# Attention and a maxout FFN on one core: groups of four heads in four 32-column TensorE tiles, 128-token output tiles, 1 KB loads, casts on GpSimd and in the weight DMA

## The chip, the cores and the metric

The kernel runs on one NeuronCore of one Trainium2 chip. The metric is the device time in microseconds (us) of one execution; medians of several executions are given. In one core's profile, PE is TensorE's matmul stream, PEld its weight loads, DVE is VectorE, ACT is ScalarE, POOL is GpSimd, SP is SyncE, which only issues DMAs here. "FFN" is the part with the weights: three up-projections, their maximum, and the output projection. "AV" is the product of the exponentials with v. A "visit" to the scores is a run of score matmuls between two runs of other matmuls: they use half of the array's 128 rows each, two at a time (row tiling), while the others use all rows, so the array changes its tiling mode on the way in and out. A column tile is a strip of 32 of the array's 128 columns. PSUM is the memory that the matmuls write (the tiles stp, av, p_i, op_ps and trT). "Streamed" means matmuls that follow one another without a wait; with 448 columns their starts are then 0.19 us apart.

## The reference

```python
# q, k, v: (8, 12, 448, 64) float32; w1, w2, w3, w_out: (768, 768) float32
scores = (1 / sqrt(64)) * q @ k.transpose(0, 1, 3, 2)
m = max(scores, axis=-1, keepdims=True)
e = exp(scores - m)
attn = e / (sum(e, axis=-1, keepdims=True) + exp(-m) + 1e-09)
x = (attn @ v).transpose(0, 2, 1, 3).reshape(8 * 448, 768)
h = maximum(maximum(x @ w1, x @ w2), x @ w3)
out = h @ w_out                       # (3584, 768) float32
```

The extra `exp(-m)` is a "1" in the denominator once the maximum is left out, as both kernels do.

## The kernel before

It takes two heads (a pair) at a time. The 448 tokens are four chunks of 112 partitions. Loads of q, k and v bring blocks of six heads in rows of 256 bytes (one head's 64 floats). All weights go through one float32 staging tile and are cast by ScalarE:

```python
wstage = ctx.enter_context(tc.tile_pool(name="wstage", bufs=1))
for i, w in enumerate((moe_w1, moe_w2, moe_w3, moe_w_out)):
    wst = wstage.tile([128, NDC, DFF], FP32, tag="wst")
    nc.sync.dma_start(out=wst, in_=w.rearrange("(dc p) f -> p dc f", p=128))
    wt = cpool.tile([128, NDC, DFF], MMDT, name=f"w{i}")
    nc.scalar.copy(out=wt, in_=wst)
```

For each pair, VectorE casts q and k, TensorE transposes them, the *previous* pair's AV product is computed (the weights are `[v | ones]`, 128 columns, so that the denominator comes out in the upper 64 rows), and then come four score visits, each of two 64-row matmuls (one head in each row half of the array). One FFN piece of the batch before is put after the first head's AV, and one after the scores:

```python
for hh in range(2):                                  # previous pair
    av = ps1.tile([128, 512], FP32, tag="bank1")
    for c in range(NCH):
        nc.tensor.matmul(out=av[:, 0:S], lhsT=v_sb[0:kk, vslot, c, :],
                         rhs=eT_all[0:kk, parq, hh, c, :], ...)
    nc.scalar.activation(out=lnd_sb, in_=av[D : 2 * D, 0:S], func=AF.Ln)
    nc.scalar.activation(out=rb_sb, in_=lnd_sb, func=AF.Exp, scale=-1.0)
    nc.vector.tensor_tensor(out=xTp_[...], in0=av[0:D, 0:S], in1=rb_sb, op=ALU.mult)
    if hh == 0:
        moe_next()
# ... cut ...
for c in range(NCH):                                 # this pair
    stp = ps2.tile([SC, 2, 512], FP32, tag="bank2")  # two buffers
    for hh in range(2):
        nc.tensor.matmul(out=stp[:, hh, 0:S], lhsT=kT2[hh*D : hh*D+D, ts(c, SC)],
                         rhs=qT2[hh*D : hh*D+D, :], start=True, stop=True)
    nc.scalar.activation(out=eT_all[0:SC, parp, :, c, :], in_=stp[:, :, 0:S],
                         func=AF.Exp, scale=scale)
moe_next()
```

## Time and profile before

| | before |
|---|---|
| time, median of 3 (range) | 471.24 us (471.17 to 475.31) |
| TensorE busy, share of the span | 419.1 us, 89% |
| one batch in the steady state | 51.76 us, of which TensorE is busy 49.97 |
| first up-projection with the third weight | 77.40 us |
| tail: from the eighth batch's first up-projection to the end | 35.7 us |

The page of the kernel before: busy time, then the span in 40 slices of 11.8 us (busy tenths, granted TensorE clock in tenths, busy tenths of the DMA engines, GB/s), then the DMA packets.

```profile
span 471.8 us, 6238 instructions
...
PE 419.1 (89%) x2400; PEld 212.3 (45%) x2400; DVE 269.6 (57%) x594; ACT 279.8 (59%) x392; POOL 0.7 (0%) x6
...
PE   2788724999999999999999999999999999998996
...
PEclk9965665999999999999999999999999999999999
...
GB/s 185 221 262 1 266 197 287 254 124 100 193 91 87 8 218 73 172 1 144 150 135 42 57 225 70 118 1 204 89 177 0 75 101 1 1 27 92 1 0 117
DMA packets 137053, 53.87 MB, mean 114 GB/s; under 512 B 130368, under 2 KB 130368, under 8 KB 137024
```

TensorE is nearly full from the eighth slice on. Before, it is busy for 42.9 of 77.4 us, much of it at half clock. Nearly all packets are under 512 bytes. The fourth slice moves 1 GB/s: the loads stand still although the weights are not yet there.

Two stretches of the kernel before, the start and one batch of the steady state (length; then busy us and instructions of PE, PEld, DVE, ACT, POOL; granted clock; DMA share; GB/s):

```profile
0.00:77.40 77.40, 42.90 (x173) 15.43 (x173) 28.58 (x68) 51.70 (x59) 0.70 (x6) 0.70 0.90 195
...
287.29:339.05 51.76, 49.97 (x302) 25.88 (x302) 33.05 (x74) 32.52 (x49) 0.00 (x0) 1.00 0.54 107
```

In the steady state no engine but TensorE is near its limit. To shorten a batch one has to take matmul time away, or the 1.8 us of idle time.

The timeline of TensorE in the kernel before, part of one pair (start, length to the modelled end of the last matmul, line, what, count, and in brackets the idle time before and what ended it):

```profile
293.60 0.59 PE L303 MATMUL stp<-qT_2789,kT_2791 64*112 64x448 f16 x4
294.12 0.93 PE L151 MATMUL p_i<-xT_b,w_112 128*128 128x448 f16 x4
295.24 0.40 PE L303 MATMUL stp<-qT_2789,kT_2791 64*112 64x448 f16 x2 [0.19 <-ACT eT_all L310]
295.56 0.55 PE L151 MATMUL p_i<-xT_b,w_112 128*128 128x448 f16 x2
295.95 0.54 PE L151 MATMUL p_i<-xT_b,w_116 128*128 128x448 f16 x2
296.50 0.40 PE L303 MATMUL stp<-qT_2789,kT_2791 64*112 64x448 f16 x2
296.82 0.93 PE L151 MATMUL p_i<-xT_b,w_116 128*128 128x448 f16 x4
```

The starts are what to read, since ends are modelled. A visit of four score matmuls takes from 293.60 to 294.12, 0.52 us, and one of two takes 0.32; streamed, a pair of them is worth 0.19. Eight matmuls need three visits here, because there are two score buffers and each must wait for its exponential (the wait in brackets). Over a batch this makes 18 or 19 visits.

The chain of waits of the kernel before, in order of time, up to the first matmul with the third weight (start, length, what):

```profile
1.17 8.13 DMA k__97<-in_k_dram
...
43.65 3.92 ACT w_112 L115
47.57 1.62 ACT eT_all L310 x2
...
60.74 3.93 ACT w_116 L115
64.69 8.60 DMA wst<-in_moe_w_dram
73.31 4.04 ACT w_120 L115
77.40 2.42 PE p_i L151 x6
```

The second weight's load is issued at 47.59 us, after the first weight's cast, which starts at 43.65, and the third's at 64.69 after the second's cast. The casts stand in ScalarE's queue behind exponentials.

### The profile page before, as it was taken

How to read it: one execution, taken by the hardware profiler on the slowest of the kernel's cores; microseconds unless marked ns; L12 is line 12 of the kernel's file. 1: busy time of each engine (PE TensorE's matmuls, PEld its weight loads, DVE VectorE, ACT ScalarE, POOL GpSimd, SP SyncE). 2: the span in 40 equal slices, each digit the busy share in tenths (PEclk: the TensorE clock that was granted, in tenths of full speed). 3: DMA queues.
4: the chain of work that ended last, by engine and by line, in shares of the span. 5: the costliest groups of instructions: out<-in, count | busy, mean ns of one | idle time of the engine just before them, and what ended most of it. 6: DMA issues, size and time to landing. Idle time of an engine off the chain costs nothing.

```text
span 471.8 us, 6238 instructions
## 1 busy us (share of the span) xinstructions
PE 419.1 (89%) x2400; PEld 212.3 (45%) x2400; DVE 269.6 (57%) x594; ACT 279.8 (59%) x392; POOL 0.7 (0%) x6
## 2 busy tenths in 40 slices
PE   2788724999999999999999999999999999998996
PEld 1222202445444554445454554456444544455454
DVE  5434322575666666656566666667566556555453
ACT  3778843766765567457855576556844776556300
POOL 0000000000000000000000000000000000000000
PEclk9965665999999999999999999999999999999999
DMA  9990979974945093906672293708490340002003
GB/s 185 221 262 1 266 197 287 254 124 100 193 91 87 8 218 73 172 1 144 150 135 42 57 225 70 118 1 204 89 177 0 75 101 1 1 27 92 1 0 117
DMA packets 137053, 53.87 MB, mean 114 GB/s; under 512 B 130368, under 2 KB 130368, under 8 KB 137024
## 3 DMA queue, kind: packets, MB, share of 16 engines
q1 hardware_dynamic: 137024, 53.48, 53.1%
q8 instruction: 18, 0.29, 0.3%
q14 instruction: 11, 0.09, 0.1%
HBM read 42.47 MB, written 11.01 MB: 113 GB/s over the span
## 4 chain that ended last, share of the span: by engine, by line
PE 74%; ACT 17%; DMA 4%; issue 3%; DVE 2%; SPq 0%; ACTq 0%
PE p_i L151 31%; PE av L272 15%; PE op_ps L172 12%; PE stp L303 12%; ACT eT_all L310 10%; ACT rb_sb L282 2%; DVE xT_b L283 2%; PE trT L242 2%; DMA wst<-in_moe_w_dram 2%; PE trT L237 2%; DMA k__97<-in_k_dram 2%; ACT lnd_sb L280 2%; ACT w_120 L115 1%; ACT w_116 L115 1%; ACT w_112 L115 1%
## 5 line engine op out<-in xcount | busy, mean ns | idle before, releaser
L310 ACT ACTIVATE eT_all<-stp 112x896 f16<-112x896 f32 x192 | 164.3, 908 | 11.1 <-PE stp L303 9.9
L280 ACT ACTIVATE lnd_sb<-av 64x448 f32<-64x448 f32 x96 | 50.5, 539 | 135.9 <-PE av L272 135.6
L283 DVE TENSOR_TENSOR xT_b<-av,rb_sb 64x448 f16<-64x448 f32 x96 | 59.0, 615 | 81.1 <-ACT rb_sb L282 80.7
L272 PE MATMUL av<-eT_all,v_sb 112*128 112x448 f16 (+1 forms) x384 | 100.6, 379 | 5.3 <-ACT eT_all L310 2.3
L161 DVE TENSOR_TENSOR hT_b<-hT_b,p_i 128x448 f16<-128x448 f16 x96 | 59.6, 620 | 40.8 <-PE p_i L151 38.0
L151 PE MATMUL p_i<-xT_b,w_120 128*128 128x448 f16 x288 | 64.6, 357 | 11.7 <-ACT w_120 L115 10.3
L172 PE MATMUL op_ps<-w_124,hT_b 128*112 128x384 f16 x384 | 73.7, 331 | 0.0
L151 PE MATMUL p_i<-xT_b,w_116 128*128 128x448 f16 x288 | 67.0, 358 | 5.1 <-ACT w_116 L115 5.1
L151 PE MATMUL p_i<-xT_b,w_112 128*128 128x448 f16 x288 | 69.5, 357 | 1.4 <-DVE xT_b L283 1.4
L172 PEld LDWEIGHTS <-hT_b 128*112 128x112 f16 x384 | 46.3, 129 | 21.7 <-issue 10.3
L282 ACT ACTIVATE rb_sb<-lnd_sb 64x448 f32<-64x448 f32 x96 | 53.3, 569 | 1.1
L272 PEld LDWEIGHTS <-v_sb 112*128 112x128 f16 (+1 forms) x384 | 34.3, 101 | 35.6 <-issue 13.9
L151 PEld LDWEIGHTS <-w_120 128*128 128x128 f16 x288 | 28.3, 99 | 40.3 <-ACT w_120 L115 11.1
L179 DVE TENSOR_SCALAR o_sb<-op_ps 112x384 f32<-112x384 f32 x64 | 35.4, 554 | 16.4 <-PE op_ps L172 14.7
L151 PEld LDWEIGHTS <-w_116 128*128 128x128 f16 x288 | 27.2, 99 | 31.9 <-ACT w_116 L115 5.4
L151 PEld LDWEIGHTS <-w_112 128*128 128x128 f16 x288 | 25.0, 98 | 30.8 <-issue 13.0
L159 DVE CAST hT_b<-p_i 128x448 f16<-128x448 f32 x48 | 29.6, 617 | 10.0 <-PE p_i L151 9.6
L115 ACT CAST w_120<-wst 128x4608 f16<-128x4608 f32 x1 | 4.0, 4032 | 8.6 <-DMA wst<-in_moe_w_dram 8.6
L237 PE MATMUL trT<-ident_86,q_133 112*128 112x112 f16 x4 | 0.9, 294 | 6.6 <-DVE q_133 L223 6.6
L229 DVE CAST k_749<-k__453 112x512 f16<-112x512 f32 x1 | 0.4, 426 | 8.3 <-DMA k__453<-in_k_dram 8.3
L75 DVE MEMSET ones_f_91<- 128x4096 f32 x1 | 3.5, 3472 | 1.7 <-PEq L336 1.7
L254 DVE TENSOR_SCALAR v_sb<-v__99 112x256 f16<-112x256 f32 x6 | 1.5, 290 | 5.0 <-PE av L272 3.9
(507 smaller groups left out, 313.6 us busy)
## 6 DMA issues: line engine op xcount, KB each, us to landing
out_dram<-o_sb SPq DMA_DIRECT2D x32, 336.0 KB, 3.1
wst<-in_moe_w_dram SPq DMA_DIRECT2D x3, 2304.0 KB, 9.7
wst<-in_moe_w_out_dram SPq DMA_DIRECT2D x1, 2304.0 KB, 8.6
q__95<-in_q_dram SPq DMA_DIRECT2D x1, 672.0 KB, 5.4
k__97<-in_k_dram SPq DMA_DIRECT2D x1, 672.0 KB, 8.1
v__99<-in_v_dram SPq DMA_DIRECT2D x1, 672.0 KB, 9.7
q__101<-in_q_dram SPq DMA_DIRECT2D x1, 672.0 KB, 9.8
k__103<-in_k_dram SPq DMA_DIRECT2D x1, 672.0 KB, 10.6
```

The source lines that it names most:

```text
L115: nc.scalar.copy(out=wt, in_=wst)
L151: nc.tensor.matmul(out=p_i[:, 0:S], lhsT=w_sb[i][:, dc, ts(fc, 128)], rhs=xTp[:, dc, :], start=(dc == 0), stop=(dc == NDC - 1),)
L159: nc.vector.tensor_copy(out=hTp[:, fc, :], in_=p_i[:, 0:S])
L161: nc.vector.tensor_tensor(out=hTp[:, fc, :], in0=hTp[:, fc, :], in1=p_i[:, 0:S], op=ALU.max)
L172: nc.tensor.matmul(out=op_ps[0:SC, 0:NW], lhsT=hTp[:, fc, ts(t, SC)], rhs=wout_sb[:, fc, ts(nh, NW)], start=(fc == 0), stop=(fc == NFC - 1),)
L179: nc.vector.tensor_scalar(out=o_sb[:, ts(nh, NW)], in0=op_ps[0:SC, 0:NW], scalar1=1.0 / LAMBDA, scalar2=None, op0=ALU.mult,)
L272: nc.tensor.matmul(out=av[:, 0:S], lhsT=v_sb[0:kk, vslot, c, :], rhs=eT_all[0:kk, parq, hh, c, :], start=(c == 0), stop=(c == NCH - 1),)
L280: nc.scalar.activation(out=lnd_sb, in_=av[D : 2 * D, 0:S], func=AF.Ln)
L282: nc.scalar.activation(out=rb_sb, in_=lnd_sb, func=AF.Exp, scale=-1.0)
L283: nc.vector.tensor_tensor(out=xTp_[(h % HD2) * D : (h % HD2) * D + D, h // HD2, :], in0=av[0:D, 0:S], in1=rb_sb, op=ALU.mult,)
L303: nc.tensor.matmul(out=stp[:, hh, 0:S], lhsT=kT2[hh * D : hh * D + D, ts(c, SC)], rhs=qT2[hh * D : hh * D + D, :], start=True, stop=True,)
L310: nc.scalar.activation(out=eT_all[0:SC, parp, :, c, :], in_=stp[:, :, 0:S], func=AF.Exp, scale=scale,)
```

## The change

The intent: use four heads together so that the AV product fits four 32-column tiles of the array, with one Ln and one Exp for four heads; load more bytes per packet; take the casts from VectorE and ScalarE.

```diff
-            out=q12_, in_=q[bb, hb*HB : (hb+1)*HB].rearrange("h (c p) d -> p (h c) d", p=SC)
+            # token p*4 + c: the four chunks of one partition are 1 KB in a row
+            out=t.rearrange("p h c d -> p h (c d)"),
+            in_=src[b].rearrange("(h g) (p c) d -> g p h (c d)", g=NG, c=NCH)[g],
 ...
-        nc.sync.dma_start(out=wst, in_=w.rearrange("(dc p) f -> p dc f", p=128))
-        nc.scalar.copy(out=wt, in_=wst)
+                nc.gpsimd.dma_start(out=w_sb[i][hh * 32 : hh * 32 + 32], in_=src[hh])  # casts
 ...
-            nc.vector.tensor_copy(out=q16, ...)          # k16 and v alike
+            nc.gpsimd.tensor_copy(out=q16, ...)
 ...
+        def col_tiled(weights):
+            bank = ps1.tile([128, 512], FP32, tag="bank1", name="av")
+            for c in range(NCH):
+                for hh in range(GH):                      # GH = 4
+                    nc.tensor.matmul(
+                        out=bank[32 * hh : 32 * hh + 32, 0:S],
+                        lhsT=weights(hh, c), rhs=eT[:, hh, c, :],
+                        start=(c == 0), stop=(c == NCH - 1))
+            return bank
+        den = col_tiled(lambda hh, c: ones16[:, :])
+        nc.scalar.activation(out=lnd, in_=den[:, 0:S], func=AF.Ln, bias=one_b)
+        nc.scalar.activation(out=rb, in_=lnd, func=AF.Exp, scale=-1.0)
+        for hf in range(2):
+            num = col_tiled(lambda hh, c: v16[:, hh, c, hf * 32 : hf * 32 + 32])
+            nc.vector.tensor_tensor(out=xT[b][:, 2*g + hf, :], in0=num[:, 0:S], in1=rb, op=ALU.mult)
 ...
+    cast_group(0)
+    for i in range(4): load_weight(i)                    # 13 DMAs issued by GpSimd
+    transpose_group(0); cast_group(1)
+    visits = [(pr, cs) for pr in range(2) for cs in ((0, 1), (2, 3))]
+        for vi, (pr, cs) in enumerate(visits):           # per group of 4 heads
+            scores_visit(i, pr, cs)                      # 4 matmuls, then 2 Exp
+            moe(per_visit)                               # an even share of FFN pieces
+            if vi == 0 and i > 0: av_group(i - 1)
+            if vi == 2 and i + 1 < NI: transpose_group(i + 1)
```

The output projection takes 128 tokens at a time over two batches (7 tiles instead of 8 of 112). Not shown in the cut: q and k of a pair leave PSUM in one VectorE copy instead of two, and casts and transposes run one group ahead.

## The prediction

> **What bounds it now.** From about 80 to 440 us the kernel repeats every 51.76 us, once per batch (chain of waits: the same up-projection at 235.54, 287.29 and 339.05 us). In one period (busy time by stretch) PE is busy 49.97 us, DVE 33.05, ACT 32.52, at full granted clock: TensorE bounds it. Streaming per batch, from that period's timeline: up-projection 108 matmuls x 0.19 us = 20.4; output 48 x 0.1625 = 7.8; AV 48 x 0.19 = 9.1; scores 24 row-tiled pairs x 0.19 = 4.6; transposes 48 x 0.05 = 2.4; sum 44.3. The other 7.4 us are short waits for exponentials (0.2 to 0.5 us) and 0.25 to 0.3 us around each of some 18 visits to the row-tiled scores. The Trainium skill (TensorEngine Tiling, Key Properties) says changing tiling mode drains TensorE; the trace agrees: a lone pair takes 0.32 us instead of 0.19.
> The start is slow: the first up-projection with the third weight begins at 77.40 us (timeline). One staging tile makes each weight wait for the ACT cast of the one before (issues at 16.5, 47.6, 64.7 us); 130368 packets are under 512 B. After the last period comes a tail of 31 us.
>
> **What changes, per batch.**
> - AV: 144 matmuls of 32 columns, in fours. If four run together: 36 x 0.2 us (the transposes already issue a load and a matmul every 0.05 us) = 7.2 instead of 9.1.
> - Output on 128 tokens: 42 matmuls, 6.8 instead of 7.8.
> - 12 score visits instead of 18, plus 3 AV visits: 15 x 0.27 = 4.1, plus 1 us of waits, instead of 7.4.
> - Period: 20.4 + 6.8 + 7.2 + 4.6 + 2.4 + 5.1 = 46.5 us. Seven periods save 37 us.
> - ACT falls to about 24.5 us per batch (6 Ln and Exp instructions, not 24), DVE to 25. Neither was critical. GpSimd: 15 casts per batch, an estimate of 10 to 20 us from DVE's 0.42 us at half to quarter speed; hidden.
>
> **Start.** Weights no longer wait for ACT or staging. About 14 MB (three weights, five groups) at 250 to 300 GB/s (peak now 287) puts the third weight at about 50 us instead of 77.
>
> **Time.** 50 + 7 x 46.5 + 34 (end of attention, tail) = 410; with stalls 412 us. Range 394 to 440. Faster by over 2%: 0.93; within 2%: 0.03; slower: 0.04.
>
> **What would show it.** The chain repeats every 46 to 47 us; 16-matmul AV blocks last 0.8 us, four starting within each 0.2 us; ACT and DVE near 200 us busy each; packets under 512 B nearly gone; first up-projection with the third weight at 45 to 60 us; no long wait on GpSimd after the start.
>
> **What would make it wrong.** Column tiles that serialise: the skill (same page, Restrictions) says column tiling disables Fast Weight Load. If one column tile's weight load waits for another tile's matmul, AV costs 27 us per batch and the kernel is slower. The skill (TensorE: Matmul & The Clock Gate, Part 3) gives 2.38x for three column tiles, so partial overlap is possible: each 0.05 us per round costs 13 us in all. Casting DMAs below 200 GB/s, or GpSimd held by issuing thirteen of them before it casts group 1, would push the start to 60 to 75 us.

## The result, and the profile after

The changed kernel takes 392.77 us (392.72 to 393.51, 3 runs) against 471.24. The ratio is 0.8314, 95% interval 0.8261 to 0.8368. Ratios in this document are the mean time of one kernel's runs over that of the other's runs of the same rounds, so not quite the ratio of the medians quoted. Executions over 1.5% slower than the fastest of the same kernel are left out of the means. Below, "before" in each set of runs was between 471.17 and 473.59 us (medians of 7 runs on the same chip).

The same parts of the page, after (slices of 9.8 us):

```profile
span 390.9 us, 7477 instructions
...
PE 363.1 (93%) x3120; PEld 180.1 (46%) x3120; DVE 174.8 (45%) x298; ACT 194.5 (50%) x241; POOL 129.7 (33%) x139
...
PE   2409999999999999999999999999999999999995
...
PEclk9999999999999999999999999999999999999998
...
GB/s 196 272 240 236 239 285 268 250 85 187 143 47 96 198 152 96 134 71 201 143 47 96 162 189 96 117 74 216 49 3 0 82 82 0 2 0 123 2 0 162
DMA packets 41202, 49.24 MB, mean 126 GB/s; under 512 B 2256, under 2 KB 37584, under 8 KB 41168
```

TensorE is full from the fourth slice on, and lost 56 us of busy time. ScalarE and VectorE lost 85 and 95 us, and GpSimd took up 129. Small packets are nearly gone.

The stretches after: the start, and two batches (the output tiles make batches alternate, so two are one period):

```profile
0.00:53.85 53.85, 30.78 (x280) 13.68 (x281) 9.24 (x18) 27.64 (x36) 33.08 (x44) 1.00 1.09 242
...
139.44:227.92 88.48, 88.48 (x783) 44.10 (x780) 43.53 (x74) 48.68 (x61) 30.36 (x31) 1.00 0.46 124
```

A batch now takes 88.48 / 2 = 44.24 us instead of 51.76, and TensorE is busy in all of it. Before, 49.97 of 51.76 were busy, so 5.7 us of the saving are matmul time (with the cost of visits in it) and 1.8 us idle time.

TensorE's timeline after, around one AV block:

```profile
236.85 0.59 PE L166 MATMUL stp<-qkT 64*112 64x448 f16 x4
237.37 1.31 PE L225 MATMUL p_i<-xT,w_113 128*128 128x448 f16 x6
238.52 1.30 PE L225 MATMUL p_i<-xT,w_114 128*128 128x448 f16 x6
239.75 0.94 PE L195 MATMUL av<-eT,ones_109 112*32 112x448 f16 x16
240.51 1.69 PE L195 MATMUL av<-eT,v_2646 112*32 112x448 f16 x32
242.13 0.59 PE L166 MATMUL stp<-qkT 64*112 64x448 f16 x4
242.65 1.31 PE L225 MATMUL p_i<-xT,w_115 128*128 128x448 f16 x6
```

The 48 AV matmuls take from 239.75 to 242.13, 2.38 us. One after another at 0.19 us they would take 9.1. In the trace four start within 10 ns (239.747, .750, .753 and .757), and the next four at 239.946: four column tiles run together. There are no brackets: nothing waits. Each score visit has four matmuls and takes 0.52 us, and there are 12 per batch.

The chain of waits after, over the start:

```profile
29.09 0.57 POOL k_0_163 L127
...
32.80 2.73 PE av L195 x43
...
35.90 6.57 ACT eT L175 x8
...
50.51 0.52 PE stp L166 x4
51.03 2.38 PE p_i L225 x12
53.40 0.52 PE stp L166 x4
53.92 2.19 PE p_i L225 x11
```

The first up-projection starts at 50.96 us, and that with the third weight at 53.85 instead of 77.40. The weights no longer stand in the chain; GpSimd's cast of the second group does, at 29.09 us. TensorE waits 13.3 us for that group's casts, because GpSimd first issues its weight DMAs (one at 1.3 us, the other twelve from 12.8 to 28.5; from the tenth of the thirteen on it waits for earlier ones to land). The granted clock of 1.00 in the line of the start above is no measurement up to 33.48 us, where the trace's first clock record stands.

**Where the 81 us of the two spans (471.8 and 390.9) went.** Reading the start of each batch's first up-projection in both traces: up to the second batch's start 125.89 against 94.22, 31.7 us (one period of 7.5 and 24 of start); six further batches 310.1 against 263.5, 46.6 us; the tail 35.7 against 33.2, 2.5 us.

### The profile page after: what moved, and what is told of

Its sections match the earlier page's. It is cut to its first block, busy times and chain, and to the rows that moved or that the text cites. A ratio compares the mean times of both kernels' runs of the same rounds, so it can differ in the third digit from the quotient of the medians.

```text
span 390.9 us, 7477 instructions
## 1 busy us (share of the span) xinstructions
PE 363.1 (93%) x3120; PEld 180.1 (46%) x3120; DVE 174.8 (45%) x298; ACT 194.5 (50%) x241; POOL 129.7 (33%) x139
## 4 chain that ended last, share of the span: by engine, by line
PE 89%; ACT 2%; POOL 0%; DVE 0%; issue 0%
PE p_i L225 43%; PE op_ps L246 15%; PE av L195 15%; PE stp L166 12%; PE trT L148 2%; PE trT L144 2%; ACT eT L175 2%; ACT rb L208 0%; POOL k_0_163 L127 0%; DVE o_sb L253 0%; ACT lnd L206 0%
## 5 line engine op out<-in xcount | busy, mean ns | idle before, releaser
L175 ACT ACTIVATE eT<-stp 112x896 f16<-112x896 f32 x192 | 164.6, 916 | 126.7 <-PE stp L166 126.7
L235 DVE TENSOR_TENSOR hT<-hT,p_i 128x448 f16<-128x448 f16 x96 | 59.7, 621 | 68.4 <-PE p_i L225 68.3
L225 PE MATMUL p_i<-xT,w_114 128*128 128x448 f16 x288 | 62.9, 353 | 0.0
L225 PE MATMUL p_i<-xT,w_113 128*128 128x448 f16 x288 | 62.8, 353 | 0.0
L225 PE MATMUL p_i<-xT,w_115 128*128 128x448 f16 x288 | 62.5, 353 | 0.0
L166 PE MATMUL stp<-qkT 64*112 64x448 f16 x384 | 60.2, 383 | 1.9 <-ACT eT L175 1.9
L246 PE MATMUL op_ps<-w_116,hT 128*128 128x384 f16 x336 | 59.0, 327 | 0.0
L211 DVE TENSOR_TENSOR xT<-av,rb 128x448 f16<-128x448 f32 x48 | 27.7, 620 | 46.3 <-ACT rb L208 46.3
L253 DVE TENSOR_SCALAR o_sb<-op_ps 128x384 f32<-128x384 f32 x56 | 31.3, 558 | 34.2 <-PE op_ps L246 34.0
L233 DVE CAST hT<-p_i 128x448 f16<-128x448 f32 x48 | 30.0, 625 | 32.6 <-PE p_i L225 32.6
L246 PEld LDWEIGHTS <-hT 128*128 128x128 f16 x336 | 30.8, 98 | 27.0 <-issue 8.1
L153 DVE COPY qkT<-trT 128x896 f16<-128x896 f16 x48 | 27.8, 617 | 29.6 <-PE trT L148 29.6
L144 PE MATMUL trT<-ident_104,q_0_162 112*128 112x112 f16 x4 | 0.9, 294 | 13.3 <-POOL q_0_162 L124 13.3
```

The source lines that it names most:

```text
L153: nc.vector.tensor_copy(out=qkT, in_=trT)
L166: nc.tensor.matmul(out=stp[:, hh, 0:S], lhsT=qkT[hh * D : hh * D + D, 1, ts(c, SC)], rhs=qkT[hh * D : hh * D + D, 0, :], start=True, stop= ...
L175: nc.scalar.activation(out=st["eT"][:, 2 * pr : 2 * pr + 2, c, :], in_=stp[:, :, 0:S], func=AF.Exp, scale=scale,)
L211: nc.vector.tensor_tensor(out=xT[b][:, 2 * g + hf, :], in0=num[:, 0:S], in1=rb, op=ALU.mult)
L225: nc.tensor.matmul(out=p_i[:, 0:S], lhsT=w_sb[i][:, dc, ts(fc, 128)], rhs=xT[b][:, dc, :], start=(dc == 0), stop=(dc == NDC - 1),)
L233: nc.vector.tensor_copy(out=dst, in_=p_i[:, 0:S])
```

## The experiments

Fifteen kernels were run. All gave correct results. The names beginning with a_ are edits of the kernel after, those with b_ of the kernel before. "Period" is the mean time per batch from the third to the seventh batch's first up-projection.

### Do four column tiles need the order of the program?

a_serial issues all four chunks of one head before the next head:

```diff
-            for c in range(NCH):
-                for hh in range(GH):
+            for hh in range(GH):
+                for c in range(NCH):
```

> The changed kernel, with the AV matmuls of one head issued in a row (head outside, chunk inside), so that neighbours use the same 32-column tile. Theory (tiles overlap because neighbours in the queue use different column tiles): an AV block of 48 grows from 2.38 us to about 48 x 0.19 = 9.1 us, and the time by 24 x 6.7 = 161 us, to about 550 us. Rival (a 32-column matmul is simply short, the order does not matter): about 393 us.

Measured: 397.94 us (one look, state unknown), period 44.35. Nothing was serialised; the 5 us more are nearly all in the start (first up-projection at 55.46 us instead of 50.96). The AV block of a_serial in TensorE's timeline:

```profile
244.68 0.97 PE L195 MATMUL av<-eT,ones 112*32 112x448 f16 x16
245.45 1.72 PE L195 MATMUL av<-eT,v 112*32 112x448 f16 x32
247.10 0.40 PE L166 MATMUL stp<-qkT 64*112 64x448 f16 x2
```

The block takes from 244.68 to 247.10, 2.42 us. The built program has the heads one after another, yet in the trace four matmuls start 13 ns apart (244.681, .695, .708 and .721), and the next at 244.881, .895, .908 and .921. Since a single column tile takes a new matmul only every 0.19 us, those four must be of different heads: a matmul that waits for its own column tile does not hold those behind it that go to other tiles. (The trace does not name the tile, so this is read from the times.) In the kernel after the four are 3 ns apart, here 13, four times as far, as four issues lie between. So the overlap does not rest on the loop order. The theory that it does fell. The rival had the time nearly right (about 393 us), but not the reason: if 32-column matmuls were simply short, they would start evenly and not in fours.

### What is the AV shape worth, and what else did it carry?

a_fullav puts back `[v | ones]` of 128 columns with Ln and Exp for each head. a_avspread does the same, but puts two heads' AV after each of two score visits instead of four heads' after one.

```diff
+        for hh in range(GH):                       # a_avspread: for hh in heads
+            av = ps1.tile([128, 512], FP32, tag="bank1", name="av")
+            for c in range(NCH):
+                nc.tensor.matmul(out=av[:, 0:S], lhsT=v16[:, hh, c, :], rhs=eT[:, hh, c, :], ...)
+            nc.scalar.activation(out=lnd, in_=av[D : 2 * D, 0:S], func=AF.Ln, bias=one_b[0:D])
+            nc.scalar.activation(out=rb, in_=lnd, func=AF.Exp, scale=-1.0)
-            if vi == 0 and i > 0: av_group(i - 1)
+            if vi < 2 and i > 0: av_group(i - 1, (2 * vi, 2 * vi + 1))      # a_avspread
```

> The changed kernel with AV as before: one 128-column matmul per head and chunk, values and ones side by side, and Ln and Exp per head on 64 partitions (8 instructions a group instead of 2). Theory (TensorE streaming bounds the period, ScalarE has room): a block is 16 x 0.19 = 3.03 us instead of 2.38, so 24 x 0.65 = 16 us more, 405 to 412 us, and no long waits for exponentials. Rival (the relief of ScalarE removed the waits of before): waits return, 3 us or more per batch on top, 430 us or more.

> a_fullav (full-width AV, Ln and Exp per head) with the four heads of a group dealt out over two score visits, two each, instead of all four in one place. ScalarE's work is the same as in a_fullav. In a_fullav the chain of waits ran through four Ln, four Exp and the exponentials queued between them once per group, and the period was about 48.4 us. Theory (not ScalarE's load but four accumulators released one after the other by its queue): period near 44.24 + 1.95 = 46.2 us, time 405 to 418 us. Rival (ScalarE's load): period stays at 48 us or more, 425 us or more.

Measured: a_fullav 434.08 us (ratio 0.9181, interval 0.9124 to 0.9237), period 48.45. a_avspread 422.26 us (0.8954, 0.8923 to 0.8986), period 46.67. The full width costs 46.67 - 44.24 = 2.43 us per batch if it is spread, and 1.78 more if eight Ln and Exp instructions stand together in ScalarE's queue: over the run TensorE waits 10.0 us for exponentials before score matmuls in a_fullav and 3.2 in a_avspread. Both times were longer than expected because the start grew too (57.8 and 59.3 us to the first up-projection). So the rival's 430 us for a_fullav came about, though with 1.78 us per batch from the queue and not 3; a_avspread came out between its theory (405 to 418) and its rival (425 or more), with a period near the theory's 46.2. The four runs of a_fullav range from 428.93 (the profiled one) to 435.84 us (the one counted as slow), so its time is less certain than its period. That the 2.43 is the width itself, the distances of starts show: AV takes 9.65 us per batch in a_avspread against 7.15 in the kernel after.

### What is a score visit worth?

a_visit1 sends one chunk per visit, 24 visits per batch instead of 12, with as many matmuls.

```diff
-    visits = [(pr, cs) for pr in range(2) for cs in ((0, 1), (2, 3))]
+    visits = [(pr, cs) for pr in range(2) for cs in ((0,), (1,), (2,), (3,))]
```

> The changed kernel with one chunk per score visit: 24 visits per batch instead of 12, one feed-forward piece after each. Theory (a visit to the row-tiled scores costs TensorE about 0.25 us beyond its streaming, whatever its length): 12 x 0.25 = 3 us per batch, period 47.2 us, time 413 to 419 us. Rival (the cost lies in waits for exponentials, which one-chunk visits do not add): below 400 us.

Measured: 414.43 us (0.8789, 0.8760 to 0.8818), period 47.17. A stretch of it, columns as before:

```profile
139.40:186.00 46.60, 46.60 (x389) 21.65 (x387) 21.52 (x37) 25.11 (x30) 14.93 (x15) 1.00 0.43 122
```

Twelve more visits cost 2.93 us, 0.244 us each, with no wait in it: TensorE is busy throughout. The Trainium skill (TensorEngine Tiling, Key Properties) says that changing the tiling mode drains TensorE; this run gives the price of one more visit, that is of a change into the mode and one out of it. By that price, six or seven fewer visits than before are worth an estimated 1.5 to 1.7 us per batch.

### Can the kernel before have the same by order alone?

b_visits puts the old score matmuls in two visits of four, with FFN pieces between. b_even also deals the FFN in 26 even pieces. b_look also casts and transposes one pair ahead.

```diff
+            scores((0, 1))          # four matmuls, then two Exp
+            moe_next()              # b_even, b_look: moe(per_visit), an even share
+            prepare(it + 1)         # b_look only: casts and transposes of the next pair
             # ... AV of the previous pair ...
-            for c in range(NCH): ...
+            scores((2, 3))
             moe_next()
```

> The kernel before, with only the order changed: scores of chunks 0 and 1, a piece of the feed-forward part, AV, then scores of chunks 2 and 3, another piece. Instructions and their sizes are unchanged, so ScalarE has the same load. Theory (visits to the scores and waits for the exponentials cost 7.4 us per batch because of the order): 12 visits instead of some 18 and nearly no waits give a period near 47.5 us instead of 51.76 and a time near 440 us (range 435 to 450). Rival (ScalarE's load makes the waits): at most 2% faster, 462 us or more.

> b_visits with the feed-forward part cut into 26 pieces (18 up-projections, 8 half output tiles) and dealt out evenly by columns over the 12 visits, as the changed kernel does; all instructions otherwise unchanged. Theory (in b_visits 5 us per batch are the last pair, which has no feed-forward left to fill the waits): the period falls from 49.4 to about 47.5 us, waits for exponentials nearly vanish, 435 to 442 us. Rival (ScalarE's load per batch, unchanged at 32 us, makes the waits): 450 us or more.

> b_even with casts and transposes done one pair ahead of their scores (six value slots instead of four), as the changed kernel does by group. Instructions and sizes per engine as in the kernel before. Theory (order alone makes the waits): period 44.3 + 12 x 0.25 = 47.3, up to 47.8 us, time 434 to 443 us. Rival (the load of ScalarE and VectorE, 32 and 33 us per batch, makes them): period 49 us or more, 450 us or more.

Measured: b_visits 452.95 us (0.9573, 0.9523 to 0.9623), period 49.44. b_even 458.22 (0.9684, 0.9626 to 0.9742), period 50.22. b_look 452.75 (0.9569, 0.9530 to 0.9608), period 49.63. Order alone is worth 2.3, 1.5 and 2.1 us per batch, and none of the three reached the 47.3 to 48 us hoped for; the times of b_even and b_look are those of their rivals (450 us or more), that of b_visits lies between its theory (435 to 450) and its rival (462 or more). In b_visits FFN work has run out by the last pair of a batch. Here is its timeline there:

```profile
315.72 0.54 PE L297 MATMUL av<-eT_all,v_sb 112*128 112x448 f16 x2
316.72 0.92 PE L297 MATMUL av<-eT_all,v_sb 112*128 112x448 f16 x4 [0.45 <-ACT eT_all L275]
```

b_even cured that and met another wait instead, 9.1 us in all before score matmuls for VectorE's copies of kT. b_look cured that too; what is left in a batch of it is 1.0 us of idle time (TensorE is busy 48.63 of 49.63) and waits shorter than 150 ns, which come up again under b_pool below.

### Where did the start come from?

b_wdma replaces staging and ScalarE's cast in the kernel before by casting DMAs; b_wdma2 holds these by a tiny copy until block 0 has landed.

```diff
-        nc.sync.dma_start(out=wst, in_=w.rearrange("(dc p) f -> p dc f", p=128))
-        nc.scalar.copy(out=wt, in_=wst)
+        nc.gpsimd.tensor_copy(out=wt[0:SC, 0, 0:8], in_=blocks[(0, 0)][2][:, 0, 0:8])  # b_wdma2 only
+        nc.gpsimd.dma_start(out=wt, in_=w.rearrange("(dc p) f -> p dc f", p=128))
```

> The kernel before, with only the weights loaded by casting DMAs from the GpSimd queue, without staging and ScalarE casts. Theory (the start of before is the chain of one staging tile): the first up-projection with the third weight moves from 77 to about 50 us, the period stays 51.76 us, the time is about 445 us (440 to 455). Rival (the start is bound by 256-byte loads): the third weight is not usable before 65 us and the time is 460 us or more.

> The kernel before with casting weight DMAs, as in b_wdma, but held back until the first block of q, k and v has landed (a tiny GpSimd copy from it into each weight tile goes ahead; its bytes are then overwritten). In b_wdma the weights, issued at 1 to 5 us, pushed the first k from 8 to 32 us. Theory (staging chain): with the first block landed first, batch 0 starts near 12 us as before, the third weight is there by about 55 us, 440 to 455 us. Rival (the start of before is bound by something else, so that the weights do not matter): 465 us or more.

Measured: b_wdma 472.66 us (0.998, 0.9933 to 1.0028): nothing gained. GpSimd issues the weights at once, and they share the DMA engines with the first loads: the first k landed after 31.9 us instead of 8.1, and VectorE stood 25.9 us for it. Both theory and rival of b_wdma had left this out, though the time is the rival's. The skill (DMA: Bandwidth & Descriptors, Issuing engines are not separate DMA queues) says just this, that DMAs of all issuers run on the same 16 engines and interleave. b_wdma2 took 460.04 us (0.972, 0.9653 to 0.9787): the same period (51.76), and a second batch that starts at 112.72 instead of 125.89, so 13.2 us of the start. That is between its theory (440 to 455 us) and its rival (465 or more). A wait of 11.0 us for v is still in it, since blocks 1 and 2 now land late.

a_load256 puts 256-byte rows back in the kernel after (in four DMAs per tensor, one per head, which is a second difference; the rows of the output go back to the order of before with it, a third).

```diff
-                in_=src[b].rearrange("(h g) (p c) d -> g p h (c d)", g=NG, c=NCH)[g],
+            rows_in = src[b].rearrange("(h g) (c p) d -> g h p c d", g=NG, c=NCH)[g]
+            for h_ in range(GH):
+                nc.sync.dma_start(out=t[:, h_], in_=rows_in[h_])
```

> The changed kernel with q, k and v loaded in 256-byte pieces as before (token order by chunk, one DMA per head); nothing else changed. Theory (in the steady part transfers are hidden, at the start they are not): period 44.2 us as before, the start later by 5 to 15 us, 398 to 408 us. Rival (load size does not matter): within 3 us of 393.

Measured: 407.61 us (0.8643, 0.8617 to 0.8669). The period is 44.24, unchanged; the first up-projection starts at 65.93 us instead of 50.96. The page of a_load256:

```profile
GB/s 156 199 199 202 206 212 194 203 203 115 185 192 93 93 176 163 92 127 105 190 107 90 93 191 146 94 93 155 146 1 2 39 117 2 2 0 109 11 0 156
DMA packets 141428, 49.27 MB, mean 121 GB/s; under 512 B 134736, under 2 KB 137808, under 8 KB 141392
```

While the start is bound by loads the DMA engines move 194 to 212 GB/s, against 236 to 285 in the kernel after. The skill (DMA: Bandwidth & Descriptors, Why small descriptors are slow) puts the fixed cost of a 256-byte packet at 3 cycles of 11, 27%; the rates here, about a fifth lower (on average 202 against 256 GB/s), agree with that order of size, though the two other differences are in them too. The steady state needs 86 to 124 GB/s and does not notice.

a_dvestart moves the casts of groups 1 to 3 and the scaling of group 0's v to VectorE, to get GpSimd out of the chain that the start shows.

```diff
-    cast_group(1)
+    cast_group(1, nc.vector, nc.vector)        # groups 2 and 3 alike; v of group 0 too
```

> The changed kernel, with the casts of groups 1 to 3 (and the values of group 0) on VectorE, so that GpSimd issues the weight DMAs without holding group 1 back (13.3 us wait of TensorE now). Theory (start bound by that wait, then by the landing of the weights at about 45 us): the first up-projection moves from 51 to about 43 to 46 us and the time to 384 to 388 us. Rival (the start is bound by the weights' landing alone): 391 to 393 us.

Measured: 407.09 us (0.8607, 0.8557 to 0.8657), worse: the first up-projection starts at 64.21 us. GpSimd, freed of casts, issued the weights from 8.6 us on instead of 12.8, so q, k and v landed later (v of the third group at 29.8 us instead of 21.9), and VectorE, whose instructions ran in the order of the program, stood before casts whose data were missing while the copies and products that TensorE needed were behind them (TensorE's longest waits for VectorE: 5.7, 4.0 and 3.8 us). Both theory and rival were wrong. The wait for GpSimd had held the weights back and kept VectorE's queue free; the run changed both at once, so it does not say which of the two mattered more.

### All of it but the matmul shapes

b_all is b_look with 1 KB loads and the held casting DMAs. b_pool is b_all with the casts of q and k and the scaling of v on GpSimd. It has what the kernel after has, except the AV and output shapes, one Ln and Exp for four heads, the joint copy of q and k, and groups of four.

```diff
-            nc.vector.tensor_copy(out=q16, ...)        # b_pool: k16 and v_sb alike
+            nc.gpsimd.tensor_copy(out=q16, ...)
```

> b_look with 1 KB loads and with casting weight DMAs held back until the first block has landed; casts stay on VectorE, AV and output tiles stay as before. Theory: period as in b_look, first up-projection of batch 0 at 50 to 58 us and of batch 1 one undisturbed period later, 415 to 425 us; what then remains to the changed kernel, 7 to 8 times about 3 us, is the matmul shapes. Rival (the casts on GpSimd or ScalarE's relief are needed too): 430 us or more.

> The kernel before with everything of the changed kernel except its matmul shapes and its joint Ln and Exp: order, pieces and look-ahead of b_look, 1 KB loads and gated casting weight DMAs of b_all, and now the casts of q and k and the scaling of v on GpSimd. Theory: the 1.8 us per batch that b_look keeps above its matmuls (49.63 against some 47.8) and b_all's late start come from VectorE's in-order queue, which holds casts that wait for loads in front of copies that TensorE needs. Then the period falls to 47.6 to 48.4 us, the first up-projection with the third weight starts below 56 us, and the time is 418 to 430 us. Rival: VectorE's load is not the reason, and what is left comes from Ln and Exp for each head in ScalarE's queue and from the batch boundary. Then the period stays 49.2 to 49.9 us and only the start moves: 430 us or more.

Measured: b_all 442.54 us (0.9354, 0.9301 to 0.9406), period 49.62; b_pool 433.30 us (0.9164, 0.9132 to 0.9196), period 49.62. One batch of the steady state of b_all, columns as before:

```profile
211.27:260.89 49.62, 48.62 (x303) 25.59 (x301) 33.12 (x74) 32.61 (x49) 0.00 (x0) 1.00 0.47 112
```

And one of b_pool:

```profile
259.60:309.20 49.60, 48.60 (x302) 25.59 (x300) 26.57 (x50) 32.62 (x48) 16.80 (x24) 1.00 0.49 117
```

And its TensorE over one pair:

```profile
260.22 1.68 PE L321 MATMUL av<-eT_all,v_sb 112*128 112x448 f16 x8
261.83 0.59 PE L288 MATMUL stp<-qT,kT 64*112 64x448 f16 x4
262.35 2.44 PE L144 MATMUL p_i<-xT_b,w 128*128 128x448 f16 x12
264.72 0.69 PE L288 MATMUL stp<-qT,kT 64*112 64x448 f16 x4
265.34 2.44 PE L144 MATMUL p_i<-xT_b,w 128*128 128x448 f16 x12
```

b_all kept its theory's period, but not its start (50 to 58 us) and time (415 to 425), which is its rival's. From b_all to b_pool VectorE lost 6.5 us of work per batch, and the period did not move. VectorE's casts are therefore not what keeps the steady state of the old shapes above its matmuls: that theory fell, and the rival's numbers fit. The casts matter at the start: the first up-projection starts at 51.19 us instead of 59.54, and TensorE's waits before transposes fall from 24.0 us, all for VectorE (15.8 for products and 8.2 for casts in its queue), to 16.1 us, 15.9 of them for GpSimd's casts.

### A kernel that beats both

a_densum sums the four chunks of exponentials on VectorE, so that the denominators need 4 matmuls instead of 16 per group. a_best does this from the fourth group on, and puts casts between the weight DMAs in GpSimd's queue.

```diff
+            add_chunks(i, pr, cs[0] // 2)          # a_best: if i >= 3
-        den = col_tiled(lambda hh, c: ones16[:, :])
+        for hh in range(GH):
+            nc.tensor.matmul(out=den[32 * hh : 32 * hh + 32, 0:S], lhsT=ones16[:, :],
+                             rhs=st["sums"][hh // 2][:, hh % 2, :], start=True, stop=True)
-    for i in range(4): load_weight(i)
-    transpose_group(0); cast_group(1)
+    load_weight(0); load_weight(1)                 # a_best only
+    transpose_group(0); cast_group(1); load_weight(2)    # w_out after group 2's casts
```

> The changed kernel, with the four chunks of exponentials added on VectorE, so that the denominators need 4 matmuls a group instead of 16. Theory (TensorE streaming bounds the period; VectorE is busy 43.5 of 88.5 us): 24 x 3 rounds x 0.19 = 13.7 us less, 377 to 383 us. Rival (VectorE's six additions a group, 0.5 to 0.9 us each, delay the copies out of PSUM): 390 us or more.

> a_densum with two mends of the start: the first three groups take denominators from all chunks (in a_densum TensorE waited 4.4 us for the sums there), and GpSimd casts group 1 after the first two weights' DMAs instead of after all four. Theory: steady saving of 1.7 us per batch kept (12 us), the first up-projection at 44 to 48 us instead of 51: 374 to 381 us. Rival (the start is bound by the bytes to be landed, in whatever order): first up-projection at 50 us or later, 380 us or more.

Measured: a_densum 388.44 us (0.8213, 0.8166 to 0.8260): the period falls to 42.53, 1.71 less, as three times 0.19 for three groups; but the first up-projection starts at 57.48 us, as TensorE waits 4.4 us at once for VectorE's sums and the start is stretched, so the time fell between theory and rival. a_best 372.95 us (0.7922, 0.7887 to 0.7957): period 42.53, first up-projection at 45.28, TensorE busy in 95% of the span. That is 20 us less than the kernel after.

## Why the prediction was right or wrong

The kernel is faster by far, as predicted, and by the predicted mechanisms. The number was too high: 412 us predicted, 392.77 measured, just below the range's lower end of 394.

**The step that failed** is the term "12 score visits instead of 18, plus 3 AV visits: 15 x 0.27 = 4.1, plus 1 us of waits", 5.1 us in the sum of 46.5. Measured in the kernel after:

| per batch, us | predicted | measured: rate from the trace times count |
|---|---|---|
| up-projection | 20.4 | 20.43 |
| output | 6.8 | 6.83 |
| AV (3 blocks of 2.38) | 7.2 | 7.14 |
| scores, streaming (24 x 0.19) | 4.6 | 4.6 |
| transposes | 2.4 | 2.4 |
| visits and waits | 5.1 | 3.0 |
| sum | 46.5 | 44.4 |

The rows add up to 0.2 us more than the 44.24 of the trace. The 3.0 is 12 x 0.52 for the visits, plus 12 x 0.11 for the slower up-projection group after each (2.38 us for twelve matmuls after a visit, 2.27 streamed), less the 4.6 of streaming; the price of a visit, 0.25, is thus near the predicted 0.27. What failed is what the term added to these twelve. The three AV blocks do not cost 0.27 each: twelve rounds at 0.19 are 2.28 of the measured 2.38, so a block's change of mode is worth 0.1, and the rounding of a round to 0.2 us had already paid for that in the term of 7.2. And the 1 us of waits did not come: TensorE is busy 88.48 of 88.48 us. This term alone is 2.1 x 7 = 15 us of the 19.

The other 4 us are small. Of the seven intervals between batches three are of the shorter kind (43.26 us) and three of the longer (45.22), and the last is only 41.34, so that they average 43.8 us and not 44.24: 3 us. The 2 us for "stalls" did not come, the tail was 33.2 instead of 34, and against them the start was 51 instead of 50 and the time is 1.8 us more than the profile's span.

**Column tiles that run together**: right. AV took 2.38 us per group with four starting within 10 ns. The skill (TensorE: Matmul & The Clock Gate, Part 3) gives 2.38 times for three tiles; here four tiles take one matmul each per 0.19 us, the time of one, so four times. The fear that the missing Fast Weight Load (TensorEngine Tiling, Restrictions) would cost time did not come true: the 32-column loads take 96 ns, about as long as the full ones with four times the columns (98), but both are hidden.

**The start**: right in its number (50 predicted; 50.96, and 53.85 for the third weight), but partly by luck. The prediction reckoned with bytes alone once staging is gone (14 MB at 250 to 300 GB/s put the third weight at 50 us). In the trace the third weight has landed at 43.5 us; what comes last before 50.96 is batch 0's own attention, at the end of the chain that runs through GpSimd's cast at 29.09. a_best, whose third weight lands at 44.7, starts at 45.28. To compare kernels with different periods, take the second batch's start less one period: before 74.1, b_look 71.1, b_wdma2 61.0, b_all 62.4, b_pool 54.4, after 50.0, a_load256 65.0. Weights without staging are worth 13 us by themselves; 256-byte loads alone lose 15 of the kernel after; GpSimd's casts are worth 8 once the rest is there. The parts overlap and do not add up, as each alone runs into the next limit. The warning about GpSimd "held by issuing thirteen of them before it casts group 1" came true (13.3 us of waiting) without pushing the start to the feared 60 to 75 us, and a_best takes 5.7 us of it back.

**The 7.5 us per batch**: 2.1 come with order alone (51.76 to 49.62, fewer visits and fewer waits). AV blocks take 2.38 x 3 = 7.14 instead of 6 x 1.61 = 9.66 in b_pool (starts 260.22 to 261.83), and output 6.83 instead of 7.8, so the shapes are worth 3.5. That leaves 7.5 - 2.1 - 3.5 = 1.9 us. Of these b_pool shows 1.0 as idle TensorE time (48.60 busy of 49.60) that the kernel after does not have, in waits for VectorE's products and maxima at the batch boundary and for exponentials before score matmuls. Read by the distances of starts, with the waits below 150 ns that the brackets leave out, most of the 1.9 lies in the score visits: 7.82 us per batch in b_pool against 6.22 in the kernel after. Of its twelve visits seven take 0.52 us as after, three take 0.62 (as that at 264.72 above), and two at the batch boundary have up to 0.6 us between the starts of their pairs. In the visit at 264.72 the second pair starts at 265.01, just after an exponential that ended at 264.96. That exponential had run late: in ScalarE's queue a head's Ln (262.23) and Exp of the reciprocal (263.60) stood before the first exponential of its visit and between the two. So here score matmuls wait for exponentials that share ScalarE's queue with each head's Ln and Exp. It is not VectorE's casts (b_pool), and not Ln and Exp for each head as such, since a_avspread keeps these, and its visits take 6.22 as after. Whether the joint Ln and Exp, the wider spacing by groups of four or the joint copy of q and k takes these waits away in the kernel after, no run separated: this part stays open.

**ScalarE and VectorE "near 200 us each"**: right for ScalarE (194.5), a little low for VectorE (174.8). Neither is near its limit in the steady state, so the 180 us less are not what shortened it; but where Ln and Exp stand in ScalarE's queue does matter (1.78 us per batch between a_fullav and a_avspread).

## What to carry to other kernels

These are lessons from this one kernel. When a stage is bound by TensorE, add up its matmuls at the streaming rate read from starts, then count the visits to another tiling mode and price one from the trace, once; here each is 0.24 us, and grouping four matmuls per visit pays where other matmuls can be put between while the exponentials run. A start that is bound by loads has several limits behind each other (packet size, staging, in-order queues that wait for data), so removing one shows little until the next is gone, and weights that are loaded too early delay what is needed first. Undo parts of a large change one at a time from the fast end as well as adding them at the slow end: the two answers differ, and the difference is the overlap.

## What the Trainium skill lacked or had wrong

- TensorE: Matmul & The Clock Gate, Part 3, says that matmuls are strictly first in, first out, without reordering. In a_serial, whose program holds one head's four matmuls before the next head's, four started at 244.681, .695, .708 and .721 us and the next four 0.2 us later, at the same 0.19 us per four as in the other order. Matmuls of different column tiles pass those that wait for their own tile. "Tiles operate independently" (TensorEngine Tiling, Key Properties) agrees with it.
- The same part has no figure for four column tiles alone. Here 16 matmuls of 112x32 by 448 start over 0.76 us, 0.19 per four.
- TensorEngine Tiling, Key Properties, tells of the drain but not its cost: 0.244 us per further visit to the row-tiled mode, in and out (a_visit1).
- GPSIMD Engine Reference, section 4.1, calls GpSimd roughly line-rate for one input. The cast of 112x512 took 0.61 us against VectorE's 0.42, and the scaling of 112x1024 to f16 2.77 us against 0.69 to 0.71 (in a_dvestart).
- DMA: Bandwidth & Descriptors tells of the engines that issuers share and of the turns that queues take on them, but has no figure for what this costs the loads that are needed first: weights issued at once made the first k land after 31.9 us instead of 8.1 (b_wdma), and a dependent copy of a few bytes that held them turned the ratio of 0.998 into 0.972 (b_wdma2).
- No page says how to read a start for which the trace has no clock record. In the kernel after the first record stands at 33.48 us, and the page prints 9 tenths for the slices before it; yet at 30 to 32 us transposes start every 0.09 us, and only later every 0.05. TensorE: Matmul & The Clock Gate, Part 1, describes a warm-up at half rate, which fits. To see the clock at a start, look at the distance of starts.
